# Squared-ReLU attention into a gated FFN: where one batch's DMA transposes and two value loads stand, and a third projection unit begun in the first batch

## The chip, the cores and the metric

The kernel runs on one core of one Trainium2 chip. The metric is the device time of one execution in microseconds; the time before is the median of three runs, 403.48 us (402.40, 403.48, 403.49). The engines are named as in the profile: PE is TensorE's matmuls and PEld its weight loads, DVE is VectorE, ACT is ScalarE, POOL is GpSimd, SP is SyncE, which here only starts transfers.

## The reference

Eight batches of twelve heads, 448 tokens, head size 64, all float32. Attention without a softmax, then a gated feed-forward layer over all 3584 tokens:

```python
scores = (q @ k.T) / sqrt(64)
attn   = maximum(scores, 0) ** 2 / 448
x      = (attn @ v)  ->  tokens x 768
gate   = maximum(x @ w_gate, 0)          # 768 -> 1536
val    = x @ w_val
out    = (gate * val) @ w_out            # 1536 -> 768
```

The kernel computes in bfloat16 with float32 accumulation.

## The kernel before

**Batches.** They are numbered 0 to 7 here, so the "seventh batch" is batch 6. Four things happen to each: its q and k are loaded and transposed; its attention runs (21 score tiles, and three times a product of squared scores with v, "values"); its x goes through the gate and value projections in 12 units; and, two batches at a time, the result goes through the output projection (`out_pair`).

**The main loop.** `first_batch` does the attention of batch 0, and with it the first steps of units 0 and 1 of batch 0's projection. Then iteration b (1 to 6) runs the 12 units of batch b - 1's projection. A unit has 12 steps of four 64 x 64 matmuls with 448 columns each; at its end ScalarE makes the gate (`g_sb`, L320) and VectorE the product `hT` (L321), which frees the unit's accumulator. The accumulators are two pairs of PSUM banks, taken in turn (`acc`), the scores and values use two others (`sc_later`). Between the steps stand events, each at a place (unit, step): score tiles and values at an even pace (`paced`), and at places written by hand the regroups, transposes, holds and loads. The order of the program on each engine is the order in which the steps and events are written; nothing reorders it. `out_pair(2)` stands between iterations 4 and 5.

From iteration 4 on attention runs ahead of the projection: iteration 4 has all of batch 4's score tiles, seven of batch 5's, and at its end batch 5's first values; iteration 5 has the rest of batch 5 and the first fourteen tiles of batch 6; iteration 6 the rest of batch 6 and all of batch 7.

**Score tiles and values.** A tile is four matmuls into a pair of banks, a ReLU on ScalarE (L232) and a square on VectorE (L233). Values are 28 matmuls, and then an eviction by ScalarE and VectorE together (L266 and L267; for batches 6 and 7 L276 and L277), and copies between partition halves (L261, L278, L279; `exchange`).

**Loading and turning a batch.** `load_qk` and `load_v` start casting loads from GpSimd's queue, four DMAs each (L116). Batches 2 to 7 are turned as follows (`turned`): VectorE copies half of k's rows into `kr`, later the other half, and the same for q into `qr` (`regroup`, L180, four copies), and after each copy SP starts two DMA transposes into the batch's `kqT` (L188, eight in all). k and q of batches 2 to 7 use one pair of buffers, `kr` and `qr` are one pair for all, and `kqT` and the v buffers are two, by the batch's parity. To keep the next loads away from running transposes, `hold(b)` makes GpSimd copy one column out of the last piece of both halves of batch b's `kqT` (L690): it waits there for the transposes, and every DMA behind it in GpSimd's queue waits too. `hold_unit` does the same on a column of `hT` (L685).

**The end of `first_batch`.** VectorE's `exchange` copies make the second (odd) x out of the first; the steps of units 0 and 1 that need it stand behind the last value passes:

```python
        value_passes(0, 2, both, 4, NC)
        exchange(0, 0)
        exchange(0, 1)
        pin(nc.scalar.activation(x_of[0][0][2], both[:, :, :S], AF.Copy))
        exchange(0, 2)
        for n in range(4):
            for u in range(2):
                passes(u, 2)
```

The functions that the change touches, with the line numbers that the profile uses:

Of the kernel before, what the change touches and what calls it, by code (L numbers as in the profile page):

```python
# [16 lines left out]
def kernel(  # L17
# [172 lines left out]
    def rotation(numbers):  # L190

        turn = [0]

        def take():
            n = numbers[turn[0] % len(numbers)]
            turn[0] += 1
            return banks[:, n:n + 2, :]
        return take
# [52 lines left out]
    def value_passes(b, qd, ps, i0, i1):  # L251

        attn, v_sb = attn_of(b, qd), v_b[b % NB]
        for i in range(i0, i1):
            mm4([ps[:, r, :S] for r in range(2)], lambda r, c: v_sb[:, 2 * qd + c, i, :],
                lambda r, c: attn[:, 2 * i + c, :], i == 0, i == NC - 1)

    def exchange(b, qd):
        x0, x1 = (x_of[b][e][qd] for e in range(2))
        for (_, p), (_, other) in zip(HALVES, HALVES[::-1]):  # L260
            pin(nc.vector.tensor_copy(x1[p], x0[other]))  # L261
# [40 lines left out]
    def gv_unit(b, mf, order, take):  # L302

        hT = hT_of[b - b % 2]
        c0 = CHUNK_OF[mf]
        w = gv_sb[c0]
        f = mf * 128 - CHUNKS[c0][0]
        col = (b % 2) * S
        o = []

        def step(n, e, hp):
            if n == 0:
                ps = take()
                o.extend(ps[:, r, :S] for r in range(2))
            x = x_of[b][e][hp // 2]
            mm4(o, lambda r, c: w[:, 2 * pair_of(b, hp) + (r ^ e), f + c * 64:f + c * 64 + 64], lambda r, c: x[:, hp % 2, :],
                n == 0, n == H - 1)
            if n == H - 1:
                g_sb = gpool.tile([128, S], BF16, name="g_sb")
                pin(nc.scalar.activation(g_sb, o[0], AF.Relu, scale=float(out_scale)))  # L320
                pin(nc.vector.tensor_tensor(hT[:, mf, col:col + S], o[1], g_sb, ALU.mult))  # L321
        return [lambda n=n, e=e, hp=hp: step(n, e, hp) for n, (e, hp) in enumerate(order)]
# [257 lines left out]
    STRAIGHT = [(e, hp) for e in range(2) for hp in range(HP)]  # L580

    BEGUN = [(e, 2 * qd + c) for qds in (range(0, 2), range(2, 3)) for e in range(2) for qd in qds for c in range(2)]
    BEGUN_IN = (4, 2)

    def gv_units(b):
        b0 = b - b % 2
        if b == b0:
            hT_of[b0] = hpool.tile([128, KF, 2 * S], BF16, name="hT")
        return [gv_unit(b, mf, BEGUN, rotation((BEGUN_IN[mf],))) if b == 0 and mf < 2 else
                gv_unit(b, mf, BEGUN if mf == 0 else STRAIGHT, acc) for mf in range(KF)]  # L590


# [16 lines left out]
    def first_batch(units):  # L609


        def passes(u, n):
            for _ in range(n):
                units[u].pop(0)()

        def bank(n):
            return banks[:, n, :]

        def tile(n, at=None):
            todo.append(tile_of(0, n, sc_first() if at is None else banks[:, at:at + 2, :]))  # L620

        todo = []

        def scored():
            relu2(*todo.pop(0))

        def second_by_dve():
            src, dst = todo.pop(1)
            r = rpool.tile([128, 2, S], BF16, name="r_sb")
            pin(nc.vector.tensor_scalar(r, src, 0.0, None, ALU.max))  # L630
            scored()
            pin(nc.vector.tensor_tensor(dst, r, r, ALU.mult))

        idle_matmuls(bank(6), 12)
        first_transposes((6, 7, 5, 4))
        idle_matmuls(bank(2), 4)
        tile(0)
        tile(1)
        both = banks[:, 6:8, :]
        for n in range(2, 19):  # L640
            tile(n)
            if n in (3, 5, 7, 9):
                hp = n // 2 + 1
                transposes(0, hp, bank(6 + hp % 2))
            if n in (12, 17):
                value_passes(0, n // 14, both, 0, NC)
            if n == 2:
                second_by_dve()
            elif n > 3:
                scored()  # L650
            if n in (12, 17):
                qd = n // 14
                pin(nc.vector.tensor_copy(x_of[0][0][qd], both[:, :, :S]))  # L653
        tile(19)
        scored()
        passes(0, 4)
        scored()
        tile(20, 0)
        scored()
        value_passes(0, 2, both, 0, 4)  # L660
        scored()
        passes(1, 4)
        value_passes(0, 2, both, 4, NC)
        exchange(0, 0)
        exchange(0, 1)
        pin(nc.scalar.activation(x_of[0][0][2], both[:, :, :S], AF.Copy))
# [4 lines that stand above are left out]
# [44 lines left out]
        return [(u, min(n, len(units[u]) - 4), e) for (u, n), e in zip(places, events)]  # L715

    def step(units, u, n, k):
        at = len(units[0]) * u + n + k
        return at // len(units[0]), at % len(units[0])

    def turned(b, units, *at):

# [30 lines left out]

    new_x(0)
    units = gv_units(0)
    first_batch(units)
    load_nat(kn_b[natural(2)], k, 2, 0, H)
    load_gv(5)
    load_nat(qn_b[natural(2)], q, 2, 0, H)
    for b in range(1, B - 1):  # L760
        if b < B - 3:
            new_x(b)
        units = units[2:] if b == 1 else gv_units(b - 1)
        last = len(units) - 1
        if b < B - 4:
            first, behind = {1: (28, 109), 2: (40, 132)}.get(b, (0, 132))
            events = paced(units, first, behind, stream(b, b + 1))
            events.append((last, 8 if b == 1 else 5, values_event(b, NQ - 1)))
        else:
            todo = [e for e in attention if e[:2] <= ENDS[b]]  # L770
            del attention[:len(todo)]
            if b == B - 4:
                begun = flat(kn_b[1], 4, S)
                x_of[b + 1] = [[begun[:, 2 * e:2 * e + 2, :]] for e in range(2)]
                del attention[[e[3] for e in attention].index(NC)]
            events = paced(units, 0, 144 if b == B - 3 else 132, todo)
            if b != B - 3:
                events.append((last, 5, values_event(*((b + 1, 0) if b == B - 4 else (B - 1, NQ - 1)))))
        if b == 1:
            events += [(1, 2 + 4 * qd, transposes_event(1, qd)) for qd in range(NQ)]  # L780
            events += turned(2, units, (last - 3, 7), (last - 2, 7))
            events += [(last, 2, lambda: (hold(2), load_v(2), load_wo(), load_qk(3)))]
        elif b == 2:
            events += [(1, 1, lambda: load_v(3))]
            events += [(last - 5 + 2 * n, 6, lambda n=n: weight_sums(2 * n)) for n in range(2)]
            events += [(last - 1 + t, 3 + 5 * h, lambda t=t, h=h: regroup(3, t, h)) for t in range(2) for h in range(2)]
            events += [(last, 10, lambda: [transpose_grouped(3, t, h) for t in range(2) for h in range(2)])]
        elif b == 3:
            events += [(2, 1, lambda: (hold_unit(2, 1), hold(3), load_qk(4), load_v(4)))]
            events += turned(4, units, (6, 1), (7, 1)) + [(8, 4, lambda: (hold(4), load_qk(5)))]  # L790
        elif b == 4:
            events += [(0, 4, lambda: load_v(5))]
            events += turned(5, units, (2, 1), (3, 1)) + [(5, 4, lambda: (hold(5), load_qk(6)))]
            events += turned(6, units, (last - 2, 6), (last - 1, 6))
        elif b == 5:
            events += [(2, 1, lambda: (hold_unit(4, 1), load_v(6), hold(6), load_qk(7)))]
            events += turned(7, units, (last - 4, 6), (last - 3, 6))
            later = [xpool.tile([128, HP, S], BF16, name=f"x{n}") for n in range(2)]
            x_of[b] = [x_of[b][e] + quads(later[e])[1:] for e in range(2)]
            x_of[B - 2] = [quads(t)[:1] for t in later]  # L800
        elif b == 6:
            events += [(3, 1, lambda: (hold(7), load_v(7)))]
            new = [xpool.tile([128, HP, S], BF16, name=f"x{n}") for n in range(2)]
            x_of[b] = [x_of[b][e] + quads(new[e])[1:] for e in range(2)]
            x_of[B - 1] = [quads(flat(t, HP, S)) for t in (kr, qr)]
        spread(units, events)
        if b == 2:
            out_pair(0, flat(kn_b[1], KH, S), [lambda: weight_sums(1), lambda: weight_sums(3)])
        elif b == 4:
            out_pair(2, flat(v_b[0], KH, S))  # L810
# [48 lines left out]
```

## Time and profile before

| | |
|---|---|
| time, median of three | 403.48 us |
| the profiled execution's own time | 403.59 us |
| its span, first to last instruction | 401.7 us |
| PE busy | 390.3 us, 97% |
| PEld busy | 288.7 us, 72% |
| DVE busy | 303.0 us, 75% |
| ACT busy | 243.6 us, 61% |
| POOL busy | 96.5 us, 24% |
| moved by DMA | 44.17 MB |
| granted TensorE clock | 1.00 throughout |

The sections of the page are: busy time by engine; the span in 40 slices; the DMA queues; the chain of work that ended last; and the costliest groups of instructions by line. Behind the page lie the timeline (start, length, engine, line, operation, and in brackets the idle time of the engine before it with what ended it), busy time by windows, and for a tile the time from a DMA's issue to its landing. "issue" as the ending of a wait means that the profile shows no instruction that ended it; a wait for the landing of a load can stand there. An engine that is marked with a q (SPq) is its queue: the time given is that of starting the transfer, not of the transfer.

Where the main parts lie in the trace: `first_batch` to about 32 us, iteration 4 from 160 to 201, `out_pair(2)` to 225, iteration 5 from 225 to 262, iteration 6 to 300.

### The profile page before, as it was taken

What the parts mean: (1) busy time and instruction counts of PE and PEld (TensorE: products, weight loads), DVE (VectorE), ACT (ScalarE), POOL (GpSimd) and SP (SyncE); (2) the same over time, 40 slices, a digit from 0 to 9 for tenths busy, and PEclk for the clock granted to TensorE, in tenths of its full rate; (3) what the DMA queues carried; (4) which work ended last, traced back from release to release, by engine and by line L of the source; (5) the groups of instructions that cost most, each with busy time, mean ns of one, the idle gap of its engine ahead of it and who ended that gap; (6) DMA issues with size and microseconds to landing.
All of it is one profiled execution on the core that took longest, in us unless ns stands there. A gap on an engine that the chain in (4) does not pass through costs nothing.

```text
span 401.7 us, 16575 instructions
## 1 busy us (share of the span) xinstructions
PE 390.3 (97%) x7376; PEld 288.7 (72%) x7376; DVE 303.0 (75%) x530; ACT 243.6 (61%) x358; POOL 96.5 (24%) x168
## 2 busy tenths in 40 slices
PE   8799999999999999999899999999999999999995
PEld 4466779978776666698577666988887766777664
DVE  5975896599944696787691478988889969997922
ACT  4962994787334776988533588899883234344231
POOL 8933301710213600503031360020003230000223
PEclk9999999999999999999999999999999999999999
DMA  9999997999936894997963588760002350000035
GB/s 149 175 196 197 197 190 94 161 205 181 127 91 170 106 164 82 156 149 87 161 116 81 160 107 104 124 86 5 3 2 51 77 154 3 2 3 3 20 89 170
DMA packets 90872, 44.17 MB, mean 110 GB/s; under 512 B 55424, under 2 KB 89792, under 8 KB 90800
## 3 DMA queue, kind: packets, MB, share of 16 engines
q0 software_dynamic: 51264, 28.83, 50.5%
q1 hardware_dynamic: 39104, 13.99, 19.7%
q8 instruction: 57, 0.93, 1.0%
q10 hardware_dynamic: 432, 0.30, 0.3%
q14 instruction: 15, 0.12, 0.1%
HBM read 47.19 MB, written 11.01 MB: 145 GB/s over the span
## 4 chain that ended last, share of the span: by engine, by line
PE 89%; DVE 4%; DMA 3%; ACT 1%; POOL 1%; issue 1%; POOLq 0%; ACTq 0%; DVEq 0%
PE ps L72 88%; DMA qn<-in_q_dram 3%; DVE attn L233 2%; ACT r_sb L232 1%; PE ps L208 1%; POOL qn L116 1%; POOL kn L116 1%; DVE kqT L209 1%; DVE hT L321 0%; DVE x L653 0%; DVE kr L180 0%; DVE x L261 0%; DVE attn L399 0%; POOL ident L112 0%; ACT g_sb L320 0%
## 5 line engine op out<-in xcount | busy, mean ns | idle before, releaser
L72 PE MATMUL ps<-x,gv 64*64 64x448 bf16 x3408 | 198.8, 349 | 1.7 <-DVE hT L321 1.2
L72 PEld LDWEIGHTS <-gv 64*64 64x64 bf16 x4032 | 147.6, 107 | 47.1 <-issue 4.2
L232 ACT ACTIVATE r_sb<-ps 128x896 bf16<-128x896 f32 x167 | 149.0, 933 | 17.2 <-PE ps L72 14.7
L233 DVE TENSOR_TENSOR attn<-r_sb 128x896 bf16<-128x896 bf16 x167 | 101.8, 622 | 28.6 <-ACT r_sb L232 21.8
L409 POOL DMA_DIRECT2D out_dram<-attn x63 | 33.1, 531 | 170.5 <-DVE attn L399 135.2
L72 PEld LDWEIGHTS <-hT 128*64 128x64 bf16 x1056 | 55.8, 110 | 21.0 <-issue 1.4
L72 PE MATMUL ps<-kqT 64*64 64x448 bf16 x672 | 66.7, 351 | 2.8 <-ACT r_sb L232 2.6
L395 ACT ACTIVATE attn<-ps 128x384 f32<-128x384 f32 (+1 forms) x64 | 28.8, 450 | 64.3 <-PE ps L72 63.3
L72 PE MATMUL ps<-wo,hT 128*64 128x384 bf16 (+1 forms) x720 | 54.3, 306 | 0.0
L321 DVE TENSOR_TENSOR hT<-ps,g_sb 128x448 bf16<-128x448 f32 x72 | 44.5, 619 | 8.9 <-ACT g_sb L320 8.2
L320 ACT ACTIVATE g_sb<-ps 128x448 bf16<-128x448 f32 x72 | 39.2, 546 | 17.9 <-PE ps L72 17.6
L399 DVE TENSOR_TENSOR attn<-ps,attn 128x384 f32<-128x384 f32 (+1 forms) x48 | 22.8, 503 | 33.0 <-ACT attn L395 18.4
L72 PEld LDWEIGHTS <-vn 64*64 64x64 bf16 (+1 forms) x888 | 35.5, 107 | 12.4 <-issue 2.3
L72 PE MATMUL ps<-attn,vn 64*64 64x448 bf16 x672 | 37.6, 350 | 0.8 <-DVE attn L233 0.8
L72 PEld LDWEIGHTS <-kqT 64*64 64x64 bf16 x672 | 26.8, 106 | 13.6 <-issue 5.2
L528 ACT ACTIVATE kqT<-ps 128x896 f32<-128x896 f32 x18 | 16.5, 918 | 25.0 <-PE ps L72 25.0
L116 POOL DMA_DIRECT2D vn<-in_v_dram x36 | 23.9, 685 | 16.6 <-PE ps L72 5.8
L72 PE MATMUL ps<-o_ring,hT 128*64 128x384 bf16 (+1 forms) x336 | 26.0, 306 | 0.0
L532 DVE TENSOR_TENSOR kqT<-ps,kqT 128x896 f32<-128x896 f32 x18 | 19.5, 1085 | 5.9 <-PE ps L72 4.2
L690 POOL COPY flag<-kqT 128x1 bf16<-128x1 bf16 x12 | 2.2, 196 | 89.6 <-DMA kqT<-kr 66.8
L261 DVE COPY x<-x 64x896 bf16<-64x896 bf16 x34 | 13.7, 402 | 2.2 <-ACT g_sb L320 0.5
L116 POOL DMA_DIRECT2D qn<-in_q_dram x20 | 14.8, 765 | 1.4 <-POOLq L843 0.8
(101 smaller groups left out, 288.6 us busy)
## 6 DMA issues: line engine op xcount, KB each, us to landing
out_dram<-attn POOLq DMA_DIRECT2D x48, 96.0 KB, 2.3
out_dram<-attn SPq DMA_DIRECT2D x48, 96.0 KB, 2.5
kn<-in_k_dram POOLq DMA_DIRECT2D x7, 384.0 KB, 7.1
qn<-in_q_dram POOLq DMA_DIRECT2D x7, 384.0 KB, 9.5
vn<-in_v_dram POOLq DMA_DIRECT2D x14, 192.0 KB, 8.9
gv<-in_moe_w_gate_dram POOLq DMA_DIRECT2D x6, 384.0 KB, 11.6
gv<-in_moe_w_val_dram POOLq DMA_DIRECT2D x6, 384.0 KB, 11.8
wo<-in_moe_w_out_dram POOLq DMA_DIRECT2D x2, 1152.0 KB, 13.5
```

The lines of the kernel that those rows point to most:

```text
L72: pin(nc.tensor.matmul(o, lhsT=l, rhs=r, start=start, stop=stop, skip_group_check=True))
L116: pin(nc.gpsimd.dma_start(out=o, in_=i))
L232: pin(nc.scalar.activation(r, src, AF.Relu))
L233: pin(nc.vector.tensor_tensor(dst, r, r, ALU.mult))
L261: pin(nc.vector.tensor_copy(x1[p], x0[other]))
L320: pin(nc.scalar.activation(g_sb, o[0], AF.Relu, scale=float(out_scale)))
L321: pin(nc.vector.tensor_tensor(hT[:, mf, col:col + S], o[1], g_sb, ALU.mult))
L395: pin(nc.scalar.activation(out_of(t, r, c), bank(P, t), AF.Copy))
L399: pin(nc.vector.tensor_tensor(o, bank(Q, t), o, ALU.add))
L409: pin(engines[c].dma_start(out=rows[:, c0:c1, :], in_=src))
L528: pin(nc.scalar.activation(held(n, j), both(PQ[n][0]), AF.Copy))
L532: pin(nc.vector.tensor_tensor(k, both(PQ[n][1]), k, ALU.add))
```

## The change

- **A third unit in the first batch.** Unit 2 of batch 0 is begun there too: it gets banks 0 and 1, takes the order of steps that begins with the first two quarters of the even x, and its first four steps stand between the last value passes and the steps that need the odd x. `sc_later` and `acc` are each turned once, so that the next to take a pair of banks takes the one that it took before. In iteration 1 unit 2 has eight steps left, so the first and last place of the paced events are lowered by four, and `step` counts by the length of the last unit.
- **Iteration 4.** Batch 5's v is no longer loaded at (0, 4) but behind `hold(5)` at (5, 4), ahead of batch 6's k and q. Batch 5's regroups and transposes move one unit later, to units 3 and 4. Batch 6's leave the iteration.
- **Iteration 5.** Batch 6's regroups and transposes stand at (0, 6) and (1, 6). The loads behind them move from (2, 1) to (3, 1), and `hold(6)` now stands ahead of batch 6's v, too, in place of `hold_unit(4, 1)`; the order is v of batch 6, then k and q of batch 7. Batch 7's regroups and transposes move one unit later, to (8, 6) and (9, 6).

```diff
-    BEGUN_IN = (4, 2)
+    BEGUN_IN = (4, 2, 0)
...
-        return [gv_unit(b, mf, BEGUN, rotation((BEGUN_IN[mf],))) if b == 0 and mf < 2 else
+        return [gv_unit(b, mf, BEGUN, rotation((BEGUN_IN[mf],))) if b == 0 and mf < len(BEGUN_IN) else
...
         value_passes(0, 2, both, 4, NC)
+        passes(2, 4)
         exchange(0, 0)
...
     def step(units, u, n, k):
-        at = len(units[0]) * u + n + k
-        return at // len(units[0]), at % len(units[0])
+        at = len(units[-1]) * u + n + k
+        return at // len(units[-1]), at % len(units[-1])
...
     first_batch(units)
+    sc_later(), acc()
...
-            first, behind = {1: (28, 109), 2: (40, 132)}.get(b, (0, 132))
+            first, behind = {1: (24, 105), 2: (40, 132)}.get(b, (0, 132))
...
         elif b == 4:
-            events += [(0, 4, lambda: load_v(5))]
-            events += turned(5, units, (2, 1), (3, 1)) + [(5, 4, lambda: (hold(5), load_qk(6)))]
-            events += turned(6, units, (last - 2, 6), (last - 1, 6))
+            events += turned(5, units, (3, 1), (4, 1)) + [(5, 4, lambda: (hold(5), load_v(5), load_qk(6)))]
         elif b == 5:
-            events += [(2, 1, lambda: (hold_unit(4, 1), load_v(6), hold(6), load_qk(7)))]
-            events += turned(7, units, (last - 4, 6), (last - 3, 6))
+            events += turned(6, units, (0, 6), (1, 6)) + [(3, 1, lambda: (hold(6), load_v(6), load_qk(7)))]
+            events += turned(7, units, (last - 3, 6), (last - 2, 6))
```

## The prediction

> **What bounds the kernel now.** The page first: TensorE is busy for 390.3 of 401.7 us and has 88% of the chain that ended last.
>
> ```profile
> span 401.7 us, 16575 instructions
> ...
> PE 390.3 (97%) x7376; PEld 288.7 (72%) x7376; DVE 303.0 (75%) x530; ACT 243.6 (61%) x358; POOL 96.5 (24%) x168
> ```
>
> So only idle TensorE time can be won or lost; the change removes no arithmetic. I asked for TensorE's busy time in steps of 10 us. Apart from the first 30 us and the tail there is one stretch below full:
>
> ```profile
> 190.00:200.00 10.00, 8.07 (x164) 5.60 (x160) 6.99 (x15) 5.91 (x9) 0.00 (x0) 1.00 1.31 173
> ```
>
> The granted clock is 1.00 there, so it is a wait. The timeline of that stretch says which (start, length, instruction, idle time before it):
>
> ```profile
> 185.94 0.19 POOL L690 COPY flag<-kqT 128x1 bf16<-128x1 bf16 x1 [5.16 <-DMA kqT<-qr]
> ...
> 186.46 1.50 POOL L116 DMA_DIRECT2D kn<-in_k_dram  x2 [0.33 <-DVE hT L321]
> ...
> 193.93 0.56 DVE L180 COPY kr<-kn 128x1536 bf16<-128x1536 bf16 x1 [2.10 <-issue]
> ...
> 196.08 1.13 PE L72 MATMUL ps<-x,gv 64*64 64x448 bf16 x18 [1.17 <-DVE hT L321]
> ...
> 197.96 0.56 DVE L180 COPY qr<-qn 128x1536 bf16<-128x1536 bf16 x1 [0.86 <-issue]
> ...
> 199.11 0.38 PE L72 MATMUL ps<-attn,vn 64*64 64x448 bf16 x4 [0.76 <-DVE attn L233]
> ```
>
> The reader should see one chain. POOL holds batch 6's loads until batch 5's transposes have landed (185.82, flag at 185.94). The k load issued at 186.46 and 187.19 lands 6.3 and 6.7 us later, at 193.85. VectorE, in order, has stood at the regroup of k since 191.83 and starts it at 193.93; the hT product behind it (L321) is late, its accumulator is not free, and TensorE stops. The same repeats for q (landed 197.88, regroup 197.96). Measured by starts: from 193.78 to 196.87 TensorE issues 36 small matmuls, which at the usual 0.189 us per four take 1.70, so 1.39 is lost; from 196.87 to 199.29 it issues 28 in 2.42 instead of 1.32: 1.10. **Together 2.49 us.** From 200 to 390 there is no other TensorE gap.
>
> **The change part by part.** Batches count from 0. "Iteration b" is a pass of the main loop; position (u, n) is step n of unit u.
>
> *Part 1, third unit begun in the first batch.* Sixteen matmuls (4 steps, 0.76 us) move from the next iteration to behind the last value passes, where VectorE's exchange copies (L261, from 25.94) are still making the odd x. The weight loads show the waits:
>
> ```profile
> 26.46 0.11 PEld L72 LDWEIGHTS <-gv 64*64 64x64 bf16 x2 [0.38 <-issue]
> 26.88 0.67 PEld L72 LDWEIGHTS <-gv 64*64 64x64 bf16 x16 [0.31 <-issue]
> ...
> 27.71 2.38 PEld L72 LDWEIGHTS <-gv 64*64 64x64 bf16 x52 [0.17 <-issue]
> ```
>
> Idle 0.38 + 0.31 + 0.17 = 0.86, less the usual 0.08 between groups of four three times: 0.62, and 0.76 of moved work covers it. I take **-0.65**, ends -0.7 and 0. Its weights landed at 25.19, before 26.2; its bank (0) was emptied by ScalarE at 25.2. The two extra bank turns and the shifted first/behind (24, 105) leave every later bank and place as it was. Cost elsewhere: batch 2's q regroup stands at 59.52 and its rows landed at 59.13, so 0.65 earlier it waits 0.2 on VectorE; that engine has such slack before TensorE needs it, and I cost it at nothing.
>
> *Part 2, iteration 4.* Batch 6's four regroups and eight transposes leave it, so the two waits above go: **-2.49**. What is late next? Batch 5's transposes move one unit later. The first regroup now follows unit 2's hT product (about 169.9 to 170.5), so SP starts at 171.05 instead of 168.56. Here is why that need not be late (SP's queue; the first pair beside the v load, the other alone):
>
> ```profile
> 168.56 7.84 SPq L188 DMA_TRANSPOSE kqT<-kr  x4
> 176.91 7.66 SPq L188 DMA_TRANSPOSE kqT<-qr  x4
> ...
> 250.28 6.07 SPq L188 DMA_TRANSPOSE kqT<-kr  x4
> 256.44 6.01 SPq L188 DMA_TRANSPOSE kqT<-qr  x4
> ```
>
> From first issue to last landing: 17.26 (168.56 to 185.82) beside batch 5's v load, which landed at 176.5; elsewhere 13.28 (from 250.28), 13.48 (55.60), 13.70 (194.55), 14.85 (144.81), 15.71 (97.29). With v behind the hold, they land at 184.3 to 186.8; batch 5's first score starts at 186.02. Nothing to 0.7; I take 0. Behind the same hold now stand v's four DMAs: hold + 0.65 (flag and first issue) + 7.5 (three v loads landed 7.35, 7.5 and 8.04 after their first issue) gives 192.5 to 195.5; the values of batch 5 need them at 196.87 - 1.39 = 195.5. Cost 0. Batch 6's k and q come 2.7 us later, with 25 us to spare.
>
> *Part 3, iteration 5.* Here a new chain is built, and it is longer than the one removed. Batch 6's regroups stand at (0,6) to (1,11), then SP's eight transposes, then POOL's hold at (3,1), then v (4 DMAs), k (2), q (2) in that order, then batch 7's regroups, moved to (8,6) to (9,11). In the clock of the trace of before:
> - VectorE's first score square of the iteration starts at 227.53, held by the output stores (2.26 idle); SP's sixteen stores end at 228.00. The regroup follows at 228.07, takes 0.55; transposes from 228.69.
> - Transposes: ends 13.28 and 15.71. Stores are still landing when they start, so I take the mean of the four that also began beside other traffic, 14.4. Landed 243.1. (Batch 6's first score stands at 242.80: 0.3 of stall, inside what follows.)
> - Hold and issue 0.65 (rows 0.54 to 0.92).
> - The loads. The trace has this very sequence v, k, q, without transposes:
>
> ```profile
> 232.86 2.69 POOL L116 DMA_DIRECT2D vn<-in_v_dram  x4 [0.34 <-PE ps L72]
> ```
>
> v lands 7.5 after that start, k at 244.38 (11.5) and q at 248.23 (15.4; its last issue at 238.09 plus 10.1). Rows of its parts give 15.15 to 15.85. So k lands at 255.3, q at 259.1.
> - Who asks for them? VectorE in the trace of before:
>
> ```profile
> 252.35 0.55 DVE L180 COPY qr<-qn 128x1536 bf16<-128x1536 bf16 x1
> ...
> 255.58 1.28 DVE L277 TENSOR_SCALAR x<-ps 64x448 bf16<-64x448 f32 x2
> ...
> 257.18 0.45 PE L72 MATMUL ps<-kqT 64*64 64x448 bf16 x4
> ```
>
> At 252.1 the changed order has k's regroup, so VectorE stands there some 3 us; at 254.3 it has q's, ahead of the eviction of batch 6's first values (L277). That eviction must free its bank before the score at 257.18. With q landed at 259.1: 0.08 to start, 0.47 for the copy, 0.55 for a square, 1.28 for L277, 0.08 to TensorE: 261.6. **+4.4** (261.6 - 257.18). The k wait (+1) lies inside it. Ends: 2.85 (13.28, 0.54, 15.15) and 6.55 (15.71, 0.92, 15.85). Later work is shifted whole: batch 7's transposes then land near 270, and its first score stands past 274.
> - The four regroups at the head of the iteration take 4 x 0.5 us of VectorE; unit 1's hT product ends at about 233.45, where unit 3 wants its bank at 233.35: 0.1, again inside the 4.4.
>
> A rule weighed at this place: the Trainium skill, "DMA: Bandwidth & Descriptors", section "Anatomy of one DMA — SWDGE (gpsimd) path", fits a load from GpSimd as 2.0 us plus its bytes at 436 GB/s. For these three tensors (2.06 MB written) that estimate is 6.7 us; the trace's 15.4 for the same DMAs disagrees, and I go by the trace. By the page's figure q would be there at 250.4 and nothing in iteration 5 would wait: the rival below.
>
> **Sum** against the profiled execution's 403.59 (span 401.7): -0.65 - 2.49 + 4.42 = +1.28, 404.87. The median of the runs shown is 403.48, 0.11 less: **404.8**. Ends of the terms: -0.65 - 2.49 + 2.85 and + 6.55, so 403.2 to 406.9.
>
> **Rivals.**
> - *The rows are there when asked for* (ends on the other side). Needed: k by 252.1 and q by 254.3, which is 4.8 us off the chain, say loads of 10.6 instead of 15.4. For it: k and q alone took 10.7 (160.29 to 171.03), so if v's transfer ran beside theirs the wait would go. Against: v lies ahead of them in POOL's order and each further 672 KB came about 3.9 us later. Time: 403.48 - 3.14 = 400.3. In between (wait partly covered): 401.5 to 403.2.
> - *Batch 5's transposes stay slow.* If the 17.26 was not owed to the v load, they land at 188.3 and TensorE stands 2.3 us at 186.02; it decides from a duration of 14.95 on. For it: q's part still took 7.66 after v had landed at 176.5. Against: five others within 15.7. Time 404.8 + 2.3 = 407.1.
> - *The removed wait comes back as a wait for v in iteration 4*: from a landing of v at 195.5 on, about 1 us per us; counted with the one above.
>
> **How the numbers follow.** Some 0.3% (1.2 us) is about what a measurement of this kernel can tell from no change: 402.3 to 404.7. The new chain as costed: 0.68, of it 0.42 above 404.7, 0.25 within, 0.01 below. Rows in time: 0.16, faster. In between: 0.06, halved between faster and same. Slow transposes or late v: 0.10, slower. Slower 0.52, same 0.28, faster 0.20. The range takes in all but the case in time and a little above: 401.5 to 407.2.
>
> **What would show it.** Right: no TensorE gap where 196.08 and 199.11 stood; batch 5's transposes in 13 to 15 us; a new VectorE idle before L180 of about 3 us and another of about 4 in iteration 5, and a TensorE gap of 3 or so at a score waiting for L277; POOL's v load of batch 6 issued some 11 us later after the output stores. Wrong: no idle time before batch 7's regroups (loads faster than 15.4, or transposes under 10), or a gap at batch 5's first score.

## The result, and the profile after

The changed kernel took **406.94 us** (median of 8 runs, 404.35 to 409.32); the kernel before, beside it on the same chip, 403.22 us (8 runs, 402.40 to 404.41). The ratio is 1.0089, with a 95% interval of 1.0062 to 1.0116: slower by 0.9%. Executions more than 1.5% above the fastest of the same kernel are left out of the ratios. The profiled execution took 406.1 us for a span of 404.3, which is 2.5 above the profiled one of before.

Where the time went is read from the traces by the starts of ReLUs (L232) of the same score tile, "(batch, tile)", in both kernels:

| stretch, between the ReLUs of | before, us | after, us | difference |
|---|---|---|---|
| (0,18) and (1,0): the end of the first batch | 17.08 | 16.59 | -0.49 |
| (2,0) and (4,0) | 87.74 | 87.52 | -0.22 |
| (4,0) and (5,7): iteration 4 and `out_pair(2)` | 64.65 | 62.08 | -2.57 |
| (5,7) and (6,14): iteration 5 | 36.64 | 42.51 | **+5.87** |
| (6,14) and (7,20): iteration 6 | 34.37 | 34.37 | 0 |

The head of the page after, with TensorE busy 1.0 us longer than before in a span that is 2.6 longer:

```profile
span 404.3 us, 16578 instructions
...
PE 391.3 (97%) x7376; PEld 282.0 (70%) x7376; DVE 302.6 (75%) x530; ACT 243.9 (60%) x358; POOL 97.0 (24%) x167
```

Busy time in windows of 10 us (columns: window, its length, then busy us and instructions of PE, PEld, DVE, ACT and POOL, granted clock, mean DMA share, GB/s):

```profile
190.00:200.00 10.00, 10.00 (x196) 6.18 (x186) 8.02 (x15) 6.58 (x11) 1.46 (x2) 1.00 1.34 169
...
240.00:250.00 10.00, 9.36 (x200) 7.24 (x204) 7.54 (x13) 7.63 (x11) 5.87 (x9) 1.00 1.01 125
250.00:260.00 10.00, 7.44 (x146) 4.96 (x139) 6.63 (x13) 5.82 (x10) 0.01 (x1) 0.97 1.09 154
260.00:270.00 10.00, 10.00 (x186) 7.25 (x182) 7.66 (x15) 7.71 (x12) 3.42 (x6) 0.86 0.79 101
```

The hole at 190 to 200 is gone: 10.00 of 10 and 196 matmuls, where before had 8.07 and 164. In its place stands a larger one at 250 to 260, with 146 matmuls. In the window behind that, TensorE is marked busy throughout and yet issues only 186 matmuls, at a granted clock of 0.86.

The new chain, in the order in which it runs. First SyncE's queue in the timeline of after (start, time of starting the transfers, engine, line, operation): batch 5's transposes and then batch 6's.

```profile
170.40 6.46 SPq L188 DMA_TRANSPOSE kqT<-kr  x4
177.37 6.25 SPq L188 DMA_TRANSPOSE kqT<-qr  x4
...
224.96 6.28 SPq L188 DMA_TRANSPOSE kqT<-kr  x4
231.33 6.25 SPq L188 DMA_TRANSPOSE kqT<-qr  x4
```

The last of batch 5's landed at 184.72, 14.32 us after the first issue, and its first score was not held up. The last of batch 6's was issued at 236.36 and landed at 240.44, which GpSimd's hold waits for (line 691 here, since the change adds a line above it):

```profile
240.55 0.19 POOL L691 COPY flag<-kqT 128x1 bf16<-128x1 bf16 x1 [5.99 <-DMA kqT<-qr]
241.11 2.68 POOL L116 DMA_DIRECT2D vn<-in_v_dram  x4 [0.37 <-PE ps L72]
243.74 1.55 POOL L116 DMA_DIRECT2D kn<-in_k_dram  x2
245.21 1.58 POOL L116 DMA_DIRECT2D qn<-in_q_dram  x2
```

From the first issue at 241.11, v landed at 248.76, k at 252.21 and q at 255.80. VectorE asks for k and q before they are there:

```profile
252.29 0.56 DVE L180 COPY kr<-kn 128x1536 bf16<-128x1536 bf16 x1 [2.29 <-DMA kn<-in_k_dram]
...
253.30 0.55 DVE L180 COPY kr<-kn 128x1536 bf16<-128x1536 bf16 x1
253.77 0.61 DVE L321 TENSOR_TENSOR hT<-ps,g_sb 128x448 bf16<-128x448 f32 x1
...
255.88 0.56 DVE L180 COPY qr<-qn 128x1536 bf16<-128x1536 bf16 x1 [0.96 <-issue]
...
256.89 1.27 DVE L277 TENSOR_SCALAR x<-ps 64x448 bf16<-64x448 f32 x2
```

And TensorE waits. The first row is batch 6's first score, which stood until the transposes had landed (240.44; the profile names L320, which had ended at 240.21). The second and third wait for what stands behind the copies:

```profile
240.64 0.38 PE L72 MATMUL ps<-kqT 64*64 64x448 bf16 x4 [0.88 <-ACT g_sb L320]
...
253.43 0.38 PE L72 MATMUL ps<-attn,vn 64*64 64x448 bf16 x4 [0.30 <-DVE attn L233]
...
258.21 0.38 PE L72 MATMUL ps<-kqT 64*64 64x448 bf16 x2 [2.26 <-DVE x L277]
...
259.39 2.49 PE L72 MATMUL ps<-x,gv 64*64 64x448 bf16 x20
```

The reader should see that the copy of q's rows (255.88) lies ahead of L277 (256.89) on VectorE, that L277 ends at 258.16, and that the score which needs its bank starts at 258.21. In the last row TensorE does not wait at all, but takes 2.49 us to the end of twenty matmuls that share it with a score tile; twenty beside a score tile took 1.12 in the kernel before at this stage's beginning (225.40 to 226.52). There the granted clock is 0.5, from 259.35 to 262.77.

### The profile page after: what moved, and what is told of

Read it like the earlier page. It is cut to its first block, busy times and chain, and to the rows that moved or that the text cites. A ratio compares the mean times of both kernels' runs of the same rounds, so it can differ in the third digit from the quotient of the medians.

```text
span 404.3 us, 16578 instructions
## 1 busy us (share of the span) xinstructions
PE 391.3 (97%) x7376; PEld 282.0 (70%) x7376; DVE 302.6 (75%) x530; ACT 243.9 (60%) x358; POOL 97.0 (24%) x167
## 4 chain that ended last, share of the span: by engine, by line
PE 87%; DMA 4%; DVE 4%; POOL 2%; issue 1%; ACT 1%; SPq 0%; POOLq 0%; DVEq 0%; ACTq 0%
PE ps L72 86%; DMA qn<-in_q_dram 3%; DVE attn L233 2%; DMA kqT<-qr 1%; PE ps L208 1%; POOL kn L116 1%; POOL qn L116 1%; DVE kqT L209 1%; DVE hT L321 0%; POOL vn L116 0%; ACT r_sb L232 0%; DVE x L277 0%; DVE x L653 0%; DVE x L267 0%; DVE qr L180 0%
## 5 line engine op out<-in xcount | busy, mean ns | idle before, releaser
L72 PEld LDWEIGHTS <-gv 64*64 64x64 bf16 x4032 | 143.1, 107 | 51.1 <-issue 2.2
L232 ACT ACTIVATE r_sb<-ps 128x896 bf16<-128x896 f32 x167 | 149.0, 933 | 21.9 <-PE ps L72 19.7
L321 DVE TENSOR_TENSOR hT<-ps,g_sb 128x448 bf16<-128x448 f32 x72 | 44.5, 619 | 8.6 <-ACT g_sb L320 8.0
L320 ACT ACTIVATE g_sb<-ps 128x448 bf16<-128x448 f32 x72 | 39.2, 546 | 17.1 <-PE ps L72 16.8
L72 PEld LDWEIGHTS <-vn 64*64 64x64 bf16 (+1 forms) x888 | 34.5, 107 | 12.9 <-issue 1.9
L528 ACT ACTIVATE kqT<-ps 128x896 f32<-128x896 f32 x18 | 16.5, 917 | 25.0 <-PE ps L72 25.0
L116 POOL DMA_DIRECT2D qn<-in_q_dram x20 | 14.8, 767 | 1.3 <-POOLq L843 0.8
```

Of the source, the lines that this page charges most:

```text
L72: pin(nc.tensor.matmul(o, lhsT=l, rhs=r, start=start, stop=stop, skip_group_check=True))
L116: pin(nc.gpsimd.dma_start(out=o, in_=i))
L232: pin(nc.scalar.activation(r, src, AF.Relu))
L528: pin(nc.scalar.activation(held(n, j), both(PQ[n][0]), AF.Copy))
```

## The experiments

Each ratio is against the kernel before on the same chip, with its 95% interval. It is formed over the executions and not from the two medians, so where executions spread it can differ from the medians' by some tenths of a percent.

**The parts alone.** Part 1 was added to the kernel before, and nothing else.

```diff
 (kernel before)
+    BEGUN_IN = (4, 2, 0)
+        passes(2, 4)            # and the five other lines of part 1
```

> The kernel before with the third unit begun in the first batch and nothing else. Theory (the moved 16 matmuls fill the wait for the odd x, and the gain stays): 0.6 us faster than before, 402.6 against 403.2, the weight loads of the third unit without idle time where 0.38, 0.31 and 0.17 stood, and batch 2's q regroup no later than 0.2 us behind its rows. Rival (the gain is given back at the next load, since batch 2's q lands when it lands): 0.0 to 0.2 us.

402.71 us against 403.27; ratio 1.0001 (0.9968 to 1.0035): the times can't tell it from no change. In the profile the effect is there. The third unit's weight loads stand among the others without the breaks of before (0.38, 0.31 and 0.17 between groups); weight loads of this kernel in the first batch:

```profile
25.91 0.11 PEld L72 LDWEIGHTS <-vn 64*64 64x64 bf16 x3 [0.30 <-issue]
25.92 5.62 PEld L72 LDWEIGHTS <-gv 64*64 64x64 bf16 x120
```

The stretch from (0,18) to (1,0) took 16.29 us here. The hole in iteration 4 is still there (8.50 of 10 us busy from 190 to 200), so part 1 has no share in its going.

**The changed kernel again**, on another chip, beside the runs that follow.

> The changed kernel once more, to set its spread beside the others. Theory (the wait of 2 to 3 us in iteration 5 is there in every execution, and in some of them the granted clock then falls to a half for 3.4 us): a median near 407, executions without the fall near 404.5, with it 406 to 409. Rival (the changed kernel's spread has to do with the chip that it ran on): the median is that of the gap-filled kernel without such a fall, 405 or less.

406.56 us (6 runs, 405.59 to 407.48) against 403.24; ratio 1.0085 (1.006 to 1.011). The same chain, with other lengths of its links: the stop is there again, and the clock stayed at 1.00 in the profiled execution. But the four executions with a mean granted clock of 0.997 and more took 405.59 to 406.72 us, not 404.5. VectorE, then TensorE, then the windows:

```profile
253.89 0.56 DVE L180 COPY kr<-kn 128x1536 bf16<-128x1536 bf16 x1 [3.73 <-DMA kn<-in_k_dram]
...
257.44 0.56 DVE L180 COPY qr<-qn 128x1536 bf16<-128x1536 bf16 x1 [0.93 <-issue]
```

```profile
255.03 0.38 PE L72 MATMUL ps<-attn,vn 64*64 64x448 bf16 x4 [1.75 <-DVE attn L233]
...
259.77 0.38 PE L72 MATMUL ps<-kqT 64*64 64x448 bf16 x2 [2.22 <-DVE x L277]
```

```profile
250.00:260.00 10.00, 6.03 (x126) 4.00 (x120) 5.31 (x11) 5.05 (x8) 0.00 (x0) 1.00 1.23 165
260.00:270.00 10.00, 9.74 (x206) 7.44 (x202) 8.84 (x17) 8.33 (x12) 2.88 (x6) 1.00 0.51 81
```

The loads took 16.11 us here, not 14.69, so the waits are longer; iteration 5 took 42.67 us, again 6.03 more than before. So a stop of nearly the same length (2.22 us) left the clock at 1.00.

**Is it the time at which the rows are asked for?** Batch 7's regroups one unit later, and nothing else.

```diff
-            events += turned(7, units, (last - 3, 6), (last - 2, 6))
+            events += turned(7, units, (last - 2, 6), (last - 1, 6))
```

> The changed kernel with batch 7's regroups and transposes one more unit later in iteration 5. Theory (the loss is that the rows of batch 7 are asked for before they land): k is asked for after its landing, q waits under 1 us, no TensorE gap over 0.6 us behind the one at batch 6's first score (0.9 to 1.0, its transposes landing late), no fall of the granted clock; 401 to 402. Rival (the loss comes from the four regroups and eight transposes at the head of iteration 5, or batch 7's transposes become the next thing that is late): 405 or more, in the second case with a gap at batch 7's first score.

402.58 us against 403.27; ratio 0.9984 (0.9966 to 1.0002). The expected 401 to 402 was missed by 0.6. Iteration 5 took 38.14 us, 1.5 more than before instead of 5.9, though the loads and batch 6's transposes stand as in the changed kernel; only batch 7's transposes moved with the copies. VectorE's wait for k is 0.75, that for q is gone:

```profile
252.52 0.56 DVE L180 COPY kr<-kn 128x1536 bf16<-128x1536 bf16 x1 [0.75 <-DMA kn<-in_k_dram]
...
253.53 1.27 DVE L277 TENSOR_SCALAR x<-ps 64x448 bf16<-64x448 f32 x2
...
257.76 0.55 DVE L180 COPY qr<-qn 128x1536 bf16<-128x1536 bf16 x1
```

L277 now comes before the copy of q, and TensorE has no gap at its score. Of the 1.5 that remain, 0.85 are two short waits for L321 (before 256.83 and 259.90, measured by the starts of the matmuls). The loss is set by who stands behind the wait, as much as by the wait's length.

**Is it the order of the loads?** k and q ahead of v.

```diff
-(hold(6), load_v(6), load_qk(7))
+(hold(6), load_qk(7), load_v(6))
```

> The changed kernel with batch 7's k and q loaded ahead of batch 6's v behind the same hold. Theory (what counts is the length of hold and three loads; whichever comes last is waited for): no idle time on VectorE before batch 7's regroups, but batch 6's first values, at 251.8, wait for v, which lands 15 us after the first issue, near 256: a TensorE gap of some 4 us, and about the changed kernel's time, 405 to 409. Rival (the loss lies in VectorE's order, where the regroups block everything behind them, and not in the loads' length): 404 or less.

406.27 us against 403.24; ratio 1.0077 (1.0047 to 1.0106). No regroup waits any more; TensorE waits for v itself, which landed at 256.16:

```profile
253.04 0.38 PE L72 MATMUL ps<-attn,vn 64*64 64x448 bf16 x2 [0.80 <-DMA vn<-in_v_dram]
255.63 1.51 PE L72 MATMUL ps<-attn,vn 64*64 64x448 bf16 x26 [2.22 <-DMA vn<-in_v_dram]
```

v, k and q are wanted within a few us of each other, and what is last in the queue is late.

**Does v in the chain cost its length?** Batch 6's v is loaded beside the transposes again, and the hold keeps only k and q back.

```diff
-[(3, 1, lambda: (hold(6), load_v(6), load_qk(7)))]
+[(1, 1, lambda: load_v(6)), (3, 1, lambda: (hold(6), load_qk(7)))]
```

> The changed kernel with batch 6's v loaded at (1, 1) of iteration 5, beside batch 6's transposes, and only k and q behind the hold. Theory (the loss is the length of the chain transposes, hold, loads): taking v's 3.5 to 4 us out of it brings k and q that much earlier, less what the transposes lose beside v (0 to 3 us): the gap at batch 6's first score grows to 1 to 4 us, the later waits shrink, and the time falls to 403.5 to 406. Rival (loads beside transposes cost what they save, as the kernel's order supposes): 406 to 408.

403.56 us against 403.33; ratio 1.0015 (0.9985 to 1.0045), some 3 us below the changed kernel. v was issued at 222.31 and landed at 231.49. The transposes, beside it for 6.4 us, took 16.16 instead of 14.8 to 15.5, and batch 6's first score waited longer; but k landed at 248.22 and q at 252.68, and no regroup waited. TensorE:

```profile
241.42 0.38 PE L72 MATMUL ps<-kqT 64*64 64x448 bf16 x4 [1.73 <-DMA kqT<-qr]
```

So putting v behind the hold saves about 0.8 us at the first score (1.73 against 0.88) and costs more than that at the regroups.

**Is the hold worth anything?** Without it, v, k and q are all loaded beside the transposes.

```diff
-(hold(6), load_v(6), load_qk(7))
+(load_v(6), load_qk(7))
```

> The changed kernel without the hold in iteration 5: v, k and q start at (3, 1), beside batch 6's transposes. Theory (the hold is the link that adds the two lengths): no wait before batch 7's regroups, the loads landed by 250, but the transposes slower, landed at 243 to 246, a gap of 3 to 6 us at batch 6's first score (due at 239.6): 404 to 407. Rival (a transfer beside the transposes hardly costs them anything, as with batch 5's v): they land by 242, and the time is 401 to 403.

411.3 us (4 runs) against 403.33; ratio 1.0205 (1.0151 to 1.0258), worse than the expectation and far from the rival's 401 to 403. The loads were issued from 222.98 on, and the transposes took 22.4 us (225.81 to 248.17). Queue, TensorE and windows:

```profile
225.81 7.70 SPq L188 DMA_TRANSPOSE kqT<-kr  x4
233.60 11.84 SPq L188 DMA_TRANSPOSE kqT<-qr  x4
```

```profile
248.37 0.59 PE L72 MATMUL ps<-kqT 64*64 64x448 bf16 x4 [7.84 <-DMA kqT<-qr]
```

```profile
240.00:250.00 10.00, 2.15 (x30) 1.11 (x26) 1.43 (x4) 1.89 (x3) 0.00 (x0) 0.66 1.07 130
250.00:260.00 10.00, 10.00 (x184) 6.29 (x180) 5.93 (x11) 6.26 (x9) 0.00 (x0) 0.83 0.01 2
```

TensorE stopped for 7.84 us, and the granted clock was 0.5 for 10.24 us (243.2 to 253.5), of which the part after 248.37 costs at half speed. The hold pays; what does not is how much stands behind it.

**Did batch 5's transposes become faster because v left?** v of batch 5 back at (0, 4), all else as changed.

```diff
+            events += [(0, 4, lambda: load_v(5))]
-(hold(5), load_v(5), load_qk(6))
+(hold(5), load_qk(6))
```

> The changed kernel with batch 5's v loaded early in iteration 4 again, so that it runs beside batch 5's transposes, which stay one unit later. Theory (the transposes take 17 us beside the load and 14 alone): first issue to last landing 16.5 to 17.5 instead of 14.3, so they land near 187.5 and TensorE stands some 2 us at batch 5's first score (185.4); 2 us above the changed kernel. Rival (their length has nothing to do with the load): 14 to 15 us again, no gap, the changed kernel's time.

406.77 us against 403.24; ratio 1.0092 (1.0064 to 1.012), the changed kernel's. The expected gap at batch 5's first score did not come. v landed at 175.46, so it ran beside the transposes for 3.9 us, and they took 13.76 (171.54 to 185.30):

```profile
171.54 5.86 SPq L188 DMA_TRANSPOSE kqT<-kr  x4
177.91 5.80 SPq L188 DMA_TRANSPOSE kqT<-qr  x4
```

In the kernel before they had run 7.9 us beside it (168.56 to 176.5) and taken 17.26. The fourteen traces hold 84 such sets of eight transposes. The 28 with at most 0.6 us of load beside them took 12.6 to 15.5 us, the 52 with 1.4 to 5.4 us of load 12.3 to 15.7; only the four with more were longer: 16.16 with 6.4 us (v beside batch 6's), 16.72 with 7.6 (part 1 alone), 17.26 with 7.9 and 22.4 with all three loads. So a few us of load beside them are not seen, and a long overlap goes with slow transposes; the sets stand in different stages, and no run varied the overlap alone. In this kernel it was enough to begin the transposes one unit later; taking v away from them added nothing.

**Is the half clock a part of the loss?** Eight matmuls on zeros, whose result nothing reads, were put ahead of the score that waits, so that TensorE does not stop for long. They write into `before[0]`, the bank pair of the score tile before.

```diff
     def scores_event(b, n):
-        return lambda: relu2(*tile_of(b, n, sc_later()))
+        def event():
+            ps = sc_later()
+            if (b, n) == (6, 10):
+                idle_matmuls(before[0][:, 0, :], 4)
+            before[:] = [ps]
+            relu2(*tile_of(b, n, ps))
+        return event
```

> The changed kernel with eight matmuls on zeros put in front of the score tile that stands 2.3 us for the eviction of batch 6's first values; they write a score bank that is free there, and nothing reads what they write. Theory (the granted clock falls to a half for 3.4 us because TensorE stands too long there, which costs some 1.7 us on top of the wait): the clock stays at 1.00 between 255 and 270 us, the score still starts at its old time, and the median is 1.5 to 2 us below the changed kernel's 406.9, near 405. Rival (the clock falls for another reason, or the fall costs nothing): the half clock is still there, or it is gone and the time is 406.9 as before.

406.6 us (10 runs, 403.4 to 408.5) against 403.27; ratio 1.0087 (1.0057 to 1.0117). The expected 405 was missed. In its profile the clock stays at 1.00; iteration 5 took 41.26 us, 1.25 less than in the changed kernel. TensorE:

```profile
258.12 0.95 PE L72 MATMUL ps<-blank 128*64 128x448 bf16 x8 [0.42 <-ACT r_sb L232]
...
259.94 0.38 PE L72 MATMUL ps<-kqT 64*64 64x448 bf16 x2 [0.57 <-DVE x L277]
```

The score still starts when L277 lets it, as it should.

The second run of the changed kernel shows a full clock without any filling, so this profile alone settles nothing. Over the executions: of the 14 of the changed kernel, 7 had a mean granted clock of 0.996 or less, and these took 407.5 us on average, the other 7 took 405.8; the kernel before was never below 0.997 in the 81 executions beside the runs of this section. Of the ten with the filling only one was at 0.996, and yet their median is no lower. What the clock costs in the median stays open: the averages suggest 1.7 us in every second execution, the filling did not win it back.

**A better place for batch 6's transposes.** The chain in iteration 5 is there because batch 6 is turned in it. First, regroups and transposes just ahead of `out_pair(2)`, with iteration 5 as before the change:

```diff
         elif b == 5:
-            events += turned(6, units, (0, 6), (1, 6)) + [(3, 1, lambda: (hold(6), load_v(6), load_qk(7)))]
-            events += turned(7, units, (last - 3, 6), (last - 2, 6))
+            events += [(2, 1, lambda: (hold_unit(4, 1), load_v(6), hold(6), load_qk(7)))]
+            events += turned(7, units, (last - 4, 6), (last - 3, 6))
...
+            for t in range(2):
+                for h in range(2):
+                    regroup(6, t, h)
+                    transpose_grouped(6, t, h)
             out_pair(2, flat(v_b[0], KH, S))
```

> The changed kernel with batch 6's regroups and transposes written just ahead of the output projection instead of behind it, and iteration 5 as it was before. Theory (the gains of the first batch and of iteration 4 are real, 0.65 + 2.5, and the whole loss is the chain transposes, hold, v, k, q, regroup in iteration 5): 400.1, no TensorE gap over 0.3 us between 190 and 390 us, batch 6's transposes landed before the output stores begin, VectorE waiting some 2 us for q at the head of the output projection with nobody waiting for it. Rival (VectorE's wait at the head of the output projection, or the transposes in front of SP's output stores, cost as much): 402 or more.

402.0 us against 403.27; ratio 0.9999 (0.9968 to 1.003). That is the rival's time and not the 400.1 expected: eight of the twelve executions took 400.70 to 402.76 us, four 404.39 to 406.62, and why is not shown, since the profiled one is the fastest (400.7). In it, neither the hole of before nor that of after is there: iteration 5 took 36.63. TensorE waits at the head of the output projection, where the four copies (198.46 to 200.5) push VectorE's sums (L349) back; iteration 4 with `out_pair(2)` took 62.72 against the changed kernel's 62.08, and the 0.17 of idle time in the row is the part of this that is marked as a wait:

```profile
204.44 2.75 PE L72 MATMUL ps<-o_ring,hT 128*64 128x384 bf16 x28 [0.17 <-DVE hT L349]
```

Then the same with the copies behind those sums:

```diff
-    def out_pair(b0, S1, extra=(), apart=None):
+    def out_pair(b0, S1, extra=(), apart=None, between=lambda: None):
...
         half_sums(S2, S1, A11, ALU.subtract, slice(0, S))
+        between()
...
-            out_pair(2, flat(v_b[0], KH, S))
+            out_pair(2, flat(v_b[0], KH, S), between=lambda: [(regroup(6, t, h), transpose_grouped(6, t, h))
+                                                              for t in range(2) for h in range(2)])
```

> As the kernel with batch 6's transposes ahead of the output projection, but with the four regroups and eight transposes written into it, behind the sums that its third product needs. Theory (what that kernel lost at 204 us, 0.6, was VectorE standing in q's regroup and copying while those sums were due): the two waits at 204 us go, 399.8 to 401.0, median some 0.6 below that kernel's 402.0. Rival (SP's output stores now stand behind the transposes, and the first square of iteration 5, which waits for a store, holds TensorE): a gap at the head of iteration 5 and 402 or more.

400.9 us against 403.24; ratio 0.996 (0.9939 to 0.9981). SyncE's queue shows the transposes running beside the output projection, all started before SyncE's own stores (the last landed at 216.72), and the two windows that had holes are full:

```profile
203.98 5.62 SPq L188 DMA_TRANSPOSE kqT<-kr  x4
209.69 5.93 SPq L188 DMA_TRANSPOSE kqT<-qr  x4
215.71 12.15 SPq L409 DMA_DIRECT2D out_dram<-attn  x16
```

```profile
190.00:200.00 10.00, 10.00 (x194) 7.45 (x184) 8.35 (x15) 6.42 (x11) 1.15 (x2) 1.00 1.32 167
...
250.00:260.00 10.00, 10.00 (x216) 7.68 (x212) 8.95 (x17) 8.94 (x14) 0.19 (x1) 1.00 0.76 111
```

Part of the rival came too. VectorE's first square of iteration 5 starts 3.4 us after its ReLU (222.62) instead of 1.3 as in the changed kernel, while SyncE is still starting stores (to 227.86); that it stands for a store is inferred, since the profile names the ReLU:

```profile
226.03 1.16 DVE L233 TENSOR_TENSOR attn<-r_sb 128x896 bf16<-128x896 bf16 x2 [3.81 <-ACT r_sb L232]
```

Against the placement ahead of the projection, the profiled executions show 0.48 won in the projection's stretch (62.24) and 0.51 lost in iteration 5 (37.14). So whether this placement is the better of the two rests on the times alone, taken on two chips.

This kernel differs from the changed one only in where batch 6 is turned and in iteration 5, and ran beside it on the same chip: 400.9 against 406.56, so these are worth 5.7 us in the times. Once more, on another chip:

> The kernel with batch 6's transposes written into the output projection once more, to stand beside the next one. Theory: 400.9 again, all executions between 400.4 and 402.9.

401.52 us against 403.33; ratio 0.9959 (0.9937 to 0.9981). Eleven executions took 400.07 to 402.92 us, one 409.6 at a mean granted clock of 0.989, so the expected spread did not hold for all. This version beats the kernel before by 0.4%, and the changed kernel, on the chip that ran both, by 1.4% in the medians. And the same without the third unit in the first batch:

> As that kernel, with the first batch as it was before (no third unit), so that only the moves of iterations 4 and 5 are left. Theory (the third unit is worth the 0.6 us that the weight loads stood idle): 401.5, 0.6 above its partner in this comparison. Rival (the first score tile of batch 1 stands 0.3 longer for VectorE in most kernels with the third unit, so that 0.3 or nothing is left of it): 0.0 to 0.3 above its partner.

401.2 us against 403.33; ratio 0.9968 (0.9942 to 0.9995), 0.3 below its partner with the third unit (401.52). The profile has (0,18) to (1,0) at 17.10 us without it and at 16.15 with it; in the times that is not seen, and neither expectation came.

## Why the prediction was right or wrong

The forecast of slower, 404.8 in a range of 401.5 to 407.2, held in sign and mechanism; slower had been given a chance of 0.52. The time came out 2.1 above the single figure, close to the upper end, and the loss, 3.7 us, is nearly three times the forecast's 1.3. The traces hold some 1.3 of the 2.1: the profiled execution took 406.1 against the sum's 404.87, by steps +0.16 in part 1, -0.08 in part 2, +1.45 in part 3, and -0.22 between (2,0) and (4,0), which no step covers. The other 0.8, from that execution to the median of 406.94, is in no trace, and its cause stays open. By its own steps:

- **Part 1, -0.65.** The idle time between the weight loads went as described. The stretch shrank by 0.49 here, and by 0.79 where part 1 stood alone; over the eleven profiles with the third unit in which no load was late there, it averages 16.5 us, against 17.1 in the two without. In the times neither comparison, with intervals of some 0.3% to each side, shows it, so 0.5 is neither confirmed nor excluded there. What the forecast left out is a stop at batch 1's first score, which waits for VectorE's L321. It is in eight of the twelve traces with the third unit, 0.17 to 0.41 us long, and in neither of the two without; in the changed kernel's:

```profile
38.74 0.38 PE L72 MATMUL ps<-kqT 64*64 64x448 bf16 x4 [0.39 <-DVE hT L321]
```

- **Part 2, -2.49.** -2.57 in the profile, and the cover named for it was there: batch 5's transposes 14.32 us (forecast 13.3 to 15.7), v landed at 192.58 (192.5 to 195.5), no wait at the first score or the values. The reason given for the transposes' length was only half right: v beside them went with slow transposes at 7.9 us in common, and not at 3.9.
- **Part 3, +4.42: the mis-sized term** (5.87 over the stage). Up to the score that waits for L277 it was right, +4.24: measured from the ReLU of (5,7), the score starts after 35.75 us (258.21 - 222.46), where the kernel before has 31.51 (257.18 - 225.67). Its links, in us (the forecast's start is 228.69 - 225.67):

| link | forecast | measured | the changed kernel again |
|---|---|---|---|
| start of batch 6's transposes, after the ReLU of (5,7) | 3.02 | 2.50 | 3.20 |
| batch 6's transposes, first issue to last landing | 14.4 | 15.48 | 14.77 |
| hold and first issue | 0.65 | 0.67 | 0.67 |
| v, k, q, first issue to q landed | 15.4 | 14.69 | 16.11 |
| q landed to the score | 2.46 | 2.41 | 2.40 |
| loss up to the score | 4.42 | 4.24 | 5.64 |

  The two long links were off by 0.4 to 1.1 us, with opposite signs in the first run and the same sign in the second: the differences of the links add up to -0.18 and +1.22. So the close agreement of the first run, 4.24 to 4.42, is partly luck. The bounds for the loads, 15.15 to 15.85, were too narrow on both sides (14.69 and 16.11). The ends of the term, added up from its own rows, are 2.94 and 6.45 and not 2.85 and 6.55; nothing hangs on that. The forecast's shape of the waits was wrong in a way that cost nothing: an idle time of about 4 us was expected before q's regroup and 0.96 was there, because the squares and the hT product that had piled up behind k's regroup ran in that time. The 4 did not follow from the forecast's own rows either: with k's regroup 3.2 late, q's would have been reached at 257.5 and waited 1.6.
- **What the sum left out** is what follows the stop. At the ReLU of (6,10), the tile that waits, the loss is 3.98 and not 4.24, since two of its four matmuls had run ahead of the stop (255.60). From there the tiles to (6,14) took 6.36 us between their ReLUs instead of 4.46, which makes 5.88 in all. Of these 1.90, about 1.7 is the half clock, 3.41 us long, in which four matmuls took 0.375 instead of 0.189; the small rest falls where matmuls follow L321 (to 260.12), pushed back too. The forecast "later work is shifted whole" failed here. In the second run the chain itself was longer and little followed; both come to about 6 (5.87 and 6.03).
- **Rivals.** The rows in time: no; the loads took 14.69 to 16.11 us, not the 10.6 at which this decides, nor the estimate of 6.7 by the fit of the Trainium skill, "DMA: Bandwidth & Descriptors", section "Anatomy of one DMA — SWDGE (gpsimd) path". Batch 5's transposes slow: no, 14.32 against the 14.95 from which it decides. v late in iteration 4: no.
- **What a measurement can tell** was put at 0.3%. Single executions of the kernel before ran from about 400 to 406 us over the study, and the intervals of the ratios were 0.2 to 0.35% to each side, with four runs up to 0.5%. The figure was about right for a dozen runs; for a median of three, as the one before was, that spread makes it too narrow.

## What to carry to other kernels

A wait in an in-order engine costs what stands behind it, so before moving transfers, follow the chain to the first instruction that asks for its last byte, and to what that engine has queued next; asking one unit later won back 4.4 of the 5.9 us here with every load unmoved (some 1.7 of the 5.9 being the half clock in that execution; against the second run it is 4.5 of 6.0). A hold that keeps loads away from transposes lengthens the chain by all that is put behind it: leave behind it only what is not wanted soon, or place the transposes in a stretch whose other work does not load. After such a stop, allow for more than its length: here 1.9 us more in one execution and 0.6 in another.

## What the runs showed of the hardware

- **A short stop may halve the granted clock for a while; where it falls matters as well as its length.** After gaps of 0.30 and 2.26 us within 5 us the clock was 0.5 for 3.41 us; after 1.75 and 2.22 us in another execution it stayed at 1.00; in and after a stop of 7.84 us it was 0.5 for 10.24 us. All stretches of one clock that a trace holds whole are multiples of 3.413 us: 3.41 and 252.59 (74 times) in the changed kernel, 10.24 (3 times) without the hold, 395.95 (116 times) in the changed kernel's second run. The Trainium skill, "TensorE: Matmul & The Clock Gate", section "Part 1: The HAM clock gate (the "warmup" mystery)", gives a free-running window of 3413 ns; these lengths agree with it.

  Counted in such windows from the first change of the clock, in all fourteen traces with their ends, the clock was 0.5 after every window in which TensorE stood for 56% of the time or more (1.49 us busy of 3.41 is the busiest of them), and never fell after one of 51% or less. (A window of 50% in the kernel without the hold left a clock that was at 0.5 where it was.) The stop of 2.26 us lies whole in one window, 255.94 to 259.35, idle for 66%. In the second run the stop of 1.75 us lies in one of 51%, and that of 2.22 us is divided by a window's end at 259.01, 43% and 30%. That is read from the traces; no run moved a stop to try it. The Trainium skill, "TensorE: Matmul & The Clock Gate", section "Why this matters for your kernels", puts the limit at idle gaps of about 3 us; here the clock fell after a stop of 2.26 us, so the measurement decides: a shorter stop can suffice, and one of 2.22 did not.
- **DMA transposes beside loads**: 80 sets of eight with up to 5.4 us of load beside them took 12.3 to 15.7 us, in nearly the same range with a load and without; the four sets with 6.4, 7.6, 7.9 and 20.7 us took 16.2, 16.7, 17.3 and 22.4.
- **The same chain of DMAs varies by over 1 us**: v, k and q landed 14.69 us after the first issue in one execution of the changed kernel and 16.11 in another; in three further kernels that keep this order behind the hold, 15.01 to 15.31.
